# Second batch's first layer: the block method twice in three of four slot pairs, its weight sums made one pair ahead, its input sums in idle tiles

## The chip, the cores and the metric

The kernel runs on one core of a Trainium2 chip. The metric is the device time of one execution in microseconds. All times below are from runs of the kernel before on that core, and times within an execution are counted from the start of its profiled span.

## The reference

Two blocks follow each other. The first is attention in which a query sees only the keys that are assigned to the same cluster:

```
mask = q_assign[:, :, :, None] == k_assign[:, :, None, :]
scores = where(mask, scale * q @ k.T, -1e9)
x = softmax(scores) @ v            # 4 batches, 8 heads, 768 rows, 64 columns
```

Its result, with the heads side by side, is a matrix x of 3072 rows and 512 columns. The second block is two layers:

```
h = x @ w_in                       # 512 x 2048
g = h * (1 / (1 + exp(-1.702 * h)))
out = g @ w_out                    # 2048 x 512
```

All data are fp32. The change concerns the first of these two layers, for the second of the four batches of 768 rows.

## The kernel before, in words

The kernel first runs the attention of all four batches, and then, batch by batch (b = 0 to 3), the first layer and the second layer. Each layer is done by a block method of Strassen's kind: a product of 2 x 2 blocks is made from seven block products instead of eight, at the price of sums of blocks of the weights, of the input and of the results. In the third and fourth batch (b = 2, 3) the method is used twice in the first layer: of the seven outer products, four are again split into 2 x 2 blocks with seven products each.

**Slots.** The first layer's 2048 columns are 16 groups of 128 (`NF`), taken as `FB` = 8 slots; slot f gives the columns of groups f and f + 8. A pair j (0 to 3, `FQ` = 4 of them) joins the slots j and j + 4. The rows of a batch are two halves of 384 (`HALF`), each two quarters of 192 (`QT`). The result lies in the tile G.

**The first batch** (b = 0) runs `first7` for each slot.

**The second batch** (b = 1) runs `first7_psum` for each slot, in the order `TURN` = 0, 4, 1, 5, 2, 6, 3, 7. It makes seven products of two matmuls of 384 columns, into three PSUM banks x, z and v. Several products are added into a bank that has been copied out just before: the third, fifth and seventh into x, the sixth into v. ScalarE copies the banks out (L942, L946, L949) and applies the gelu (`finish`, L936); VectorE adds (`add`, L884). ScalarE's order in a slot is: copy of the first product, copy of the third, gelu of g1[0] (which needs VectorE's add of z), copy of v, gelu of g2[1] (which needs VectorE's add of x), and so on. Between the slots VectorE makes the weight sums of a later slot (`sums_w1`, three sums of 256 columns) and, after each second slot, the eight sums that the method needs a second time for a whole pair (`inner_w`). These are not used in this batch; they are written to DRAM (`kept_i`, four transfers, 1.5 MB for each pair) for the two batches that follow. `after7` makes a difference of two results and, for the second slot of a pair, `start_t`, the first input sums of the second layer, in the tiles Y11, E0, E1 and E2.

**The third and fourth batch** run `first49`. For each pair j it makes three outer products with full halves (`whole`, products 1, 6 and 7, four matmuls of 384 columns each, in two banks of the pool of two named m) and seven inner products (`inner`, four matmuls of 192 columns each, in six banks b: two each of z, x and v). Inner products go in the order 2, 1, 5, 6, 3, 7, 4; the adds of 3 and 7 are VectorE's, the copies of the others ScalarE's. The order of everything is written out by hand in the loop over j: the wholes of pair j − 1 stand between the inner products of pair j, except in the first pair, which has all three wholes of its own at its start, and the last, which has its own at its end. Weight sums come from `kept_i` through `load_inner` into the tiles Zb; the sixteen sums of the input M are made first of all, on VectorE. The function hands back a generator `rest`, two steps that are run in the first block of the second layer.

**What sets the order.** The instruction order of each engine is the order of the program text. Each engine takes its instructions in that order, and the SP queue its transfers. Small steps are woven between others with generators: `do(steps, n)` runs the next n steps. `pend` holds three steps that turn the previous batch's result (two VectorE transposes each, into E0, E1 and E2) and store it (four transfers each).

**The second layer** (`second49`, seven blocks k) uses weight sums `W[k]`, each of three transfers of 256 KB from `kept_w` (`load_sums`), in a pool of two buffers. `load_sums(0)` and `load_sums(1)` for the second batch are issued in the blocks 5 and 6 of the first.

Of the kernel before, what the change touches and what calls it, by code (L numbers as in the profile page):

```python
# [38 lines left out]
def fast(  # L39
# [789 lines left out]
    def load_sums(k, made=False):  # L829
        W[k] = ws.tile([P, 3, FQ, P], FP32, name="Wz")  # L830
        if made:
            keep_w(k, [W[k][:, i] for i in range(3)], nc.vector)
            return
        for i in range(3):
            nc.sync.dma_start(out=W[k][:, i], in_=kept_w[k, i])
# [86 lines left out]
    def first7_psum(b, f, X, T):  # L922

        S = w_of.pop(b * FB + f)

        def product(ps, a, x, start=True):
            for c in range(2):
                nc.tensor.matmul(out=ps, lhsT=a[:, c], rhs=x(c),  # L928
                                 start=start and c == 0, stop=(c == 1),
                                 skip_group_check=True)  # L930

        def bank_b():
            return ps_b.tile([P, 512], FP32, name="b")[:, 0:HALF]

        def finish(g, ps=None):
            nc.scalar.activation(out=g, in_=g if ps is None else ps,  # L936
                                 func=AF.Gelu_apprx_sigmoid, scale=2.0)

        g1, g2 = G[:, f], G[:, f + FB]
        x, z, v = (bank_b() for _ in range(3))  # L940
        product(x, A_in(0, 0, f), lambda c: X[0, 0, c])
        nc.scalar.copy(g1[:, 0], x)  # L942
        product(z, A_in(0, 1, f), lambda c: X[1, 0, c])
        add(g1[:, 0], z, g1[:, 0])
        product(x, S[2], lambda c: T[2, c], False)
        nc.scalar.copy(g1[:, 1], x)  # L946
        finish(g1[:, 0])
        product(v, S[1], lambda c: T[1, c])
        nc.scalar.copy(g2[:, 1], v)  # L949
        product(x, S[3], lambda c: T[3, c], False)  # L950
        add(g2[:, 1], x, g2[:, 1])
        finish(g2[:, 1])
        product(v, S[4], lambda c: X[1, 1, c], False)
        add(g1[:, 1], v, g1[:, 1])
        finish(g1[:, 1])
        product(x, A_in(1, 1, f), lambda c: T[4, c], False)
        finish(g2[:, 0], x)
# [19 lines left out]
    def sums_w1(n):  # L977

        if n >= FB:
            return  # L980
        f = TURN[n]
        if n not in range(2, 6):
            S = wq.tile([P, 3, 2, P], FP32, name="W")
        else:
            S = Zb[1 + n // 2 % 2][:, n % 2 * 6:n % 2 * 6 + 6].rearrange(
                "p (i c) n -> p i c n", c=2)
        w_of[FB + f] = {1: S[:, 0], 2: S[:, 1], 3: A_in(1, 0, f), 4: S[:, 2],
                        0: S}
        S = w_of[FB + f]
        A11, A12, A22 = A_in(0, 0, f), A_in(0, 1, f), A_in(1, 1, f)  # L990
        sums(nc.gpsimd if n < 2 else nc.vector, (
            (S[2], A22, "-", S[3]), (S[1], S[2], "+", A11),
            (S[4], A12, "-", S[2])))

    def inner_w(j, S):

        st = Zb[4]
# [9 lines left out]
        for n, (a, s3) in enumerate(((of_s, st[:, 0:2]),  # L1007
                                     (of_w, of_w(1, 0)))):
            s2, s1, s4 = (st[:, i:i + 2] for i in range(2 + 6 * n, 8 + 6 * n, 2))
            sums(nc.vector, ((s3, a(0, 0), "-", a(1, 0)),  # L1010
                             (s2, a(1, 1), "-", s3),
                             (s1, s2, "+", a(0, 0)),
                             (s4, a(0, 1), "-", s2)))
        for at, x in ((slice(0, 14), st[:, 0:14]),
                      (slice(14, 20), S[0].rearrange("p i c n -> p (i c) n")),
                      (slice(20, 22), S[1][:, 1]),
                      (slice(22, 24), S[1][:, 0:3:2, 1])):
            nc.sync.dma_start(out=kept_i[j, :, at], in_=x)

# [10 lines left out]
    def first49(X, T):  # L1030
# [5 lines left out]
        rooms = [tq[:, i] for i in range(2)]  # L1036
        for _ in range(2):
            r = wq.tile([P, 3, 2, P], FP32, name="W").rearrange(
                "p i c n -> p (i c n)").rearrange("p (n t) -> p n t", t=QT)
            rooms += [r[:, i] for i in range(4)]  # L1040
        rooms += [ep.tile([P, QT], FP32, name="p5") for _ in range(2)]
        M = {}
        for o in b:
            M[o] = {1: b[o][0, 0], 2: b[o][1, 0], 3: b[o][1, 1],
                    7: b[o][0, 1], **{n: rooms.pop(0) for n in (6, 5, 4)}}
        for todo in ((2, 5), (3, 4)):
            for n, one, op, two in ((7, 3, "-", 7), (6, 7, "+", 1),
                                    (5, 3, "-", 6)):
                for o in todo:
                    sums(nc.vector, ((M[o][n], M[o][one], op, M[o][two]),))  # L1050
        for o in b:
            sums(nc.vector, ((M[o][4], M[o][2], "-", M[o][6]),))

# [18 lines left out]
        def whole(j, n):  # L1072
# [3 lines left out]
            for m in range(2):  # L1076
                f = j + m * FQ
                at = j % 2 * 8 + m * 4
                a = {1: A_in(0, 0, f), 6: Zb[4][:, at:at + 2],
# [22 lines left out]
        def inner(j, n):  # L1102
# [7 lines left out]
            def a(o):  # L1110
# [7 lines left out]
                elif o == 5:  # L1118
                    known = {1: K[:, 14], 2: K[:, 15], 4: L[:, 6], 7: K[:, 0]}
                    s2 = 2  # L1120
                else:
                    known = {1: L[:, 2], 2: L[:, 3], 4: L[:, 7], 7: K[:, 1]}
                    s2 = 3
# [33 lines left out]

        end = FQ - 1
        for j in range(FQ):
            if j == 0:  # L1160
                whole(0, 1)
                inner(0, 2)
                p1 = keep_whole(0)
                whole(0, 6)
                u2 = keep_whole(0)
                inner(0, 1)
                do(pend, 3)
                whole(0, 7)
            else:
# [3 lines left out]
                if j > 1:  # L1173
                    whole(j - 1, 6)
                    add_whole(j - 1, 0, 1)
                load_inner(j + 1, (1,))
            inner(j, 5)
            if j < end:
                inner(j, 6)
            if j:  # L1180
                if j > 1:
# [7 lines left out]
            if j:  # L1189
# [5 lines left out]
            inner(j, 7)  # L1195
            if j == end:
                whole(j, 6)
                u2 = keep_whole(j)
            elif j:
                whole(j, 1)  # L1200
            inner(j, 4)
            if j == end:
                whole(j, 7)
            load_inner(j + 2, (0,))
# [3 lines left out]
            if j:  # L1208
                add_whole(j, 0, 0)
                close(j - 1)  # L1210
            else:
                for h, o in enumerate((p1, u2)):
                    g = quarter(0, 0, h)
# [162 lines left out]

    oks = {}
    pend = iter(())
    for b in range(B):
        if b == 1:  # L1380
            done = None
            for n, f in enumerate(TURN):
                made_w = w_of[FB + f][0]
                first7_psum(b, f, *XT)
                if n % 2 == 0 and done:
                    inner_w(*done)
                sums_w1(n + 2)
                if n:
                    after7(TURN[n - 1])
                if n % 2 == 0:  # L1390
                    one = made_w
                else:
                    done = f - FQ, (one, made_w)
                do(pend, 2)
            after7(FB - 1)
            inner_w(*done)
        if b > 1:
            rest = first49(*XT)
# [41 lines left out]
        def chain(*todo):  # L1440
            for steps in todo:
                yield from steps

# [6 lines left out]
        if b < 2:  # L1450
            rest = iter(())

        for k in range(7):
# [19 lines left out]
            if k < 5:  # L1473
                load_sums(k + 2, b == 0 and k > 2)
            elif b < B - 1:
# [452 lines left out]
```

## Time and profile before

| what | us |
|---|---|
| median of 3 runs (888.67 to 888.92) | 888.7 |
| the profiled execution | 888.23 |
| its span, first to last instruction | 886.1 |
| second batch's first layer, from the first L928 matmul to the first L1254 matmul | 476.21 to 549.78 |
| second batch's second layer | 549.9 to 613.6 |
| third batch's first layer | 613.48 to 681.11 |
| third batch's second layer | 681.2 to 744.9 |

The page is that of one execution. PE is TensorE, PEld its weight loads, DVE VectorE, ACT ScalarE, POOL GpSimd, and SP the engine that issues most transfers. A matmul in fp32 has two records, each with its own weight load. The matmuls' ends are modelled and overlap the next one's start, so that the distance between starts, and not the printed length, is what a matmul costs. A bracket after a timeline line gives how long the engine was idle before it, and what ended that idle time.

### The profile page before, as it was taken

To read this page: it belongs to the slowest core of one execution; us is meant where nothing else is said; L and a number is where in the kernel's file an instruction comes from. 1 tells how busy PE (TensorE), PEld (TensorE's weight loads), DVE (VectorE), ACT (ScalarE), POOL (GpSimd) and SP (SyncE) were. 2 spreads that over 40 slices of the span, in tenths; PEclk is the share of its full clock that TensorE was granted. 3 is DMA by queue.
4 is the path that set the end of the run, shared out by engine and by line. 5 is a ranking of instruction groups with operands and counts; after the bars stand their busy time and mean duration, and the time that the engine had idled before them with its cause. 6 is when DMAs were issued, how large, how long until landed. Compare 5 with 4: busy or idle time off the path is not lost.

```text
span 886.1 us, 18197 instructions
## 1 busy us (share of the span) xinstructions
PE 873.0 (99%) x6910; PEld 604.4 (68%) x6910; DVE 727.3 (82%) x1241; ACT 394.5 (45%) x868; POOL 430.9 (49%) x393
## 2 busy tenths in 40 slices
PE   8999999999999999999999999999999999999996
PEld 3444444444444445557997556999888998887996
DVE  4899899999999996999798556799666899665994
ACT  3677777777677774222112333111444212444211
POOL 6899999999999998695220000134000143000120
PEclk9999999999999999999999999999999999999999
DMA  9755566665656220024643321747501547501523
GB/s 172 136 107 106 104 121 137 137 147 128 137 131 136 87 68 19 0 107 143 221 150 112 103 93 71 285 144 268 170 26 48 171 145 260 173 25 48 187 65 99
DMA packets 183185, 110.48 MB, mean 125 GB/s; under 512 B 153528, under 2 KB 161712, under 8 KB 180528
## 3 DMA queue, kind: packets, MB, share of 16 engines
q1 hardware_dynamic: 182832, 109.09, 45.5%
q8 instruction: 57, 0.93, 0.5%
q14 instruction: 40, 0.33, 0.1%
q10 hardware_dynamic: 256, 0.13, 0.1%
HBM read 83.05 MB, written 26.14 MB: 123 GB/s over the span
## 4 chain that ended last, share of the span: by engine, by line
PE 95%; DVE 2%; DMA 1%; SPq 1%; ACT 0%; issue 0%; POOL 0%; DVEq 0%; ACTq 0%
PE b L1254 29%; PE s L492 14%; PE o L557 14%; PE b L1129 8%; PE b L893 8%; PE m L1084 7%; PE b L928 6%; PE s L515 3%; PE m L574 3%; PE m L348 1%; DVE Z L618 1%; DMA in<-in_q_dram 1%; SPq L134 0%; DMA short<-in_centroids_dram 0%; DVE G L884 0%
## 5 line engine op out<-in xcount | busy, mean ns | idle before, releaser
L541 POOL TENSOR_TENSOR sum<-sum,A 128x384 f32<-128x384 f32 x252 | 265.2, 1087 | 23.2 <-ACT A L523 21.5
L618 POOL TENSOR_TENSOR Y<-y,Y 128x768 f32<-128x768 f32 x24 | 59.8, 2503 | 384.8 <-DVE y L884 357.5
L523 ACT ACTIVATE A<-s 128x768 f32<-128x768 f32 x192 | 146.0, 807 | 86.0 <-PE s L515 64.7
L492 PE MATMUL s<-T,T 64*64 64x384 f32 x1536 | 143.1, 487 | 0.0
L557 PE MATMUL o<-A,inv 64*64 64x384 f32 x1536 | 141.2, 483 | 0.0
L884 DVE TENSOR_TENSOR G<-b,G 128x384 f32<-128x384 f32 x128 | 68.4, 554 | 52.5 <-PE b L928 29.3
L492 PEld LDWEIGHTS s<-T,T 64*64 64x64 f32 x1536 | 54.9, 132 | 69.1 <-ACT A L523 35.8
L618 DVE TENSOR_TENSOR G<-G 128x768 f32<-128x768 f32 (+1 forms) x84 | 99.3, 1209 | 0.2
L557 PEld LDWEIGHTS o<-A,inv 64*64 64x64 f32 x1536 | 58.3, 133 | 38.4 <-issue 33.3
L1254 PE MATMUL b<-G,w_out 128*128 128x192 f32 x320 | 55.9, 326 | 0.0
L1142 ACT COPY G<-b 128x384 f32<-128x384 f32 x64 | 30.4, 479 | 52.2 <-PE b L1129 52.2
L1254 PEld LDWEIGHTS b<-G,w_out 128*128 128x128 f32 x320 | 52.7, 190 | 1.1
L1254 PE MATMUL b<-E,Wz 128*128 128x192 f32 x288 | 50.3, 326 | 0.0
L1254 PEld LDWEIGHTS b<-E,Wz 128*128 128x128 f32 x288 | 47.3, 190 | 0.3 <-DVE E L618 0.3
L515 PE MATMUL s<-rows,rows 64*64 64x384 bf16 x720 | 45.4, 322 | 0.0
L515 PEld LDWEIGHTS <-rows 64*64 64x64 bf16 x720 | 23.0, 107 | 32.7 <-issue 32.7
L1254 PE MATMUL b<-G,Wz 128*128 128x192 f32 x224 | 41.0, 326 | 0.0
L1254 PE MATMUL b<-G,Z 128*128 128x192 f32 x224 | 39.0, 326 | 0.0
L541 POOL TENSOR_TENSOR sum<-A 128x384 f32<-128x384 f32 x32 | 37.3, 1185 | 0.0
L1254 PEld LDWEIGHTS b<-G,Wz 128*128 128x128 f32 x224 | 37.2, 190 | 0.0
L898 ACT ACTIVATE G<-G 128x384 f32<-128x384 f32 x32 | 16.1, 523 | 46.5 <-DVE G L884 45.1
L1254 PEld LDWEIGHTS b<-G,Z 128*128 128x128 f32 x224 | 36.8, 190 | 0.0
(237 smaller groups left out, 1681.1 us busy)
## 6 DMA issues: line engine op xcount, KB each, us to landing
Wz<-kept_w SPq DMA_DIRECT2D x78, 256.0 KB
Z<-kept_z SPq DMA_DIRECT2D x9, 1024.0 KB
raw<-in_moe_w_in_dram SPq DMA_DIRECT2D x16, 512.0 KB
raw<-in_moe_w_out_dram SPq DMA_DIRECT2D x16, 512.0 KB
Z<-kept_i SPq DMA_DIRECT2D x8, 1024.0 KB
inv<-in_v_dram SPq DMA_DIRECT2D x16, 384.0 KB
in<-in_q_dram SPq DMA_DIRECT2D x60, 96.0 KB
in<-in_k_dram SPq DMA_DIRECT2D x60, 96.0 KB
```

The lines of the kernel that those rows point to most:

```text
L492: nc.tensor.matmul(out=ps[c:c + D, a, 0:HALF], lhsT=T[p, 1][rows, kt * P + c:kt * P + c + D], rhs=T[p, 0][rows, h * HALF:(h + 1) * HALF], ...
L515: nc.tensor.matmul(out=s_of[u][c:c + D, a, :], lhsT=rows_of[1, p % 2][rows, kt * P + c:kt * P + c + D], rhs=rows_of[0, p % 2][rows, h * HA ...
L523: nc.scalar.activation(out=A_of[u], in_=s_of.pop(u), func=AF.Exp, scale=SCALE)
L541: nc.gpsimd.tensor_tensor(out=sum_of[g][:, a], in0=(A_of[u - 1] if kt == 1 else sum_of[g])[:, a], in1=A_of[u][:, a], op=ALU.add)
L557: nc.tensor.matmul(out=o_of[g][a * D:(a + 1) * D, r, 0:HALF], lhsT=v_in[p][rows, a, kt, :], rhs=A[rows, a, :], start=(kt == 0), stop=(kt = ...
L618: engine.tensor_tensor(out=o, in0=a, in1=b, op=(ALU.add if op == "+" else ALU.subtract))
L884: nc.vector.tensor_tensor(out=o, in0=p, in1=a, op=ALU.add)
L893: nc.tensor.matmul(out=ps[:, 0:HALF], lhsT=a[:, c], rhs=x(c), start=(c == 0), stop=(c == 1))
L928: nc.tensor.matmul(out=ps, lhsT=a[:, c], rhs=x(c), start=start and c == 0, stop=(c == 1), skip_group_check=True)
L1084: nc.tensor.matmul(out=whole_of[j][m][:, 0:HALF], lhsT=a[:, c], rhs=x(c), start=n == 1 and c == 0, stop=c == 1, skip_group_check=True)
L1129: nc.tensor.matmul(out=ps[i][:, h * QT:(h + 1) * QT], lhsT=a(o), rhs=M[o][n], start=n in (1, 2, 5) and h == 0, stop=True, skip_group_check ...
L1254: nc.tensor.matmul(out=ps, lhsT=A[n][:, f], rhs=M[n][:, f], start=start and f == 0, stop=(f == FQ - 1), skip_group_check=True)
```

## The change

In the second batch only the slots 0 and 4 are still made by `first7_psum`. The pairs 1, 2 and 3 are made by `first49`, which now takes the first pair `j0`, the input sums `M`, the weight sums `own` and background steps `bg`.

- **Weight sums.** `make_w(j)` makes the three sums of each of the pair's two slots (six of 256 columns; for pair 0 they exist) and the eight inner ones, and writes them to `kept_i` with the same four transfers. It is a generator with a step after each sum. The sums of pair j + 1 are made during pair j: `back` runs two steps after each inner product and the rest at the pair's end. Those of pair 1 are made during the slots 0 and 4, those of pair 0, which only later batches need, during pair 3. Their places are Y12 and Y21, or Zb[4], for the slots' sums, and Zb[1] or Zb[2] for the inner ones.
- **First two slots.** `first7_psum` calls a hook after the matmuls of each product, ahead of that product's add. The hook runs two steps of a chain: `pend`, `make_w(1)`, and the sixteen input sums (`sums_m`). What is left of the chain is run after the second slot.
- **Input sums.** They lie in the tile of W[1], which is taken in the first batch's last block but not loaded there, in Y22, in tq and in two p5 tiles. `load_sums(1)` is issued after the first layer.
- **Rest.** The second batch's second layer now runs the `rest` steps in its first block, as the later batches do.

The diff, cut to its core:

```diff
-    def first7_psum(b, f, X, T):
+    def first7_psum(b, f, X, T, hook):
...
                                  start=start and c == 0, stop=(c == 1),
                                  skip_group_check=True)
+            hook()
...
-        sums(nc.gpsimd if n < 2 else nc.vector, (
-            (S[2], A22, "-", S[3]), (S[1], S[2], "+", A11),
-            (S[4], A12, "-", S[2])))
-
-    def inner_w(j, S):
-
-        st = Zb[4]
+    def sums_s(f, S, engine):
+
+        A11, A12, A22 = A_in(0, 0, f), A_in(0, 1, f), A_in(1, 1, f)
+        for o, x, op, y in ((S[:, 1], A22, "-", A_in(1, 0, f)),
+                            (S[:, 0], S[:, 1], "+", A11),
+                            (S[:, 2], A12, "-", S[:, 1])):
+            sums(engine, ((o, x, op, y),))
+            yield
+
+    def make_w(j):
+
+        if j == 2:
+            own[j] = [Zb[4][:, m * 6:m * 6 + 6].rearrange(
+                "p (i c) n -> p i c n", c=2) for m in range(2)]
+        elif j:
+            own[j] = [Y[n].rearrange("p a t -> p (a t)").rearrange(
+                "p (i c n) -> p i c n", c=2, n=P) for n in (12, 21)]
+        S, st = own[j], Zb[1 if j == 0 else 1 + j % 2]
+        for m in range(2 if j else 0):
+            yield from sums_s(j + m * FQ, S[m], nc.vector)
...
+            for one in ((s3, a(0, 0), "-", a(1, 0)), (s2, a(1, 1), "-", s3),
+                        (s1, s2, "+", a(0, 0)), (s4, a(0, 1), "-", s2)):
+                sums(nc.vector, (one,))
+                yield
...
-    def first49(X, T):
+    def first49(X, T, M, own, bg, j0):
...
+        def back(j, n=2):
+            if own:
+                do(bg[j], n)
...
-        for j in range(FQ):
+        for j in range(j0, FQ):
+            first, late = j == j0, j > j0 + 1
...
+            back(j)
             inner(j, 5)
+            back(j)
             if j < end:
                 inner(j, 6)
+                back(j)
...
             inner(j, 3)
+            back(j)
...
             inner(j, 7)
+            back(j)
...
             inner(j, 4)
+            back(j)
...
+            back(j, 16)
...
         if b == 1:
-            done = None
-            for n, f in enumerate(TURN):
-                made_w = w_of[FB + f][0]
-                first7_psum(b, f, *XT)
-                if n % 2 == 0 and done:
-                    inner_w(*done)
-                sums_w1(n + 2)
-                if n:
-                    after7(TURN[n - 1])
-                if n % 2 == 0:
-                    one = made_w
-                else:
-                    done = f - FQ, (one, made_w)
-                do(pend, 2)
-            after7(FB - 1)
-            inner_w(*done)
+            M = {}
+            rooms = in_rooms(W[1].rearrange("p i f n -> p (i f n)")) + in_rooms(
+                Y[22].rearrange("p m t -> p (m t)")) + more_rooms()
+            bg = {j: make_w(j + 1) for j in range(1, FQ - 1)}
+            bg[FQ - 1] = make_w(0)
+            bg[0] = chain(pend, make_w(1), sums_m(*XT, rooms, M))
+            for f in (0, FQ):
+                first7_psum(b, f, *XT, lambda: do(bg[0], 2))
+            after7(0)
+            do(bg[0], 40)
+            after7(FQ)
+            rest = first49(*XT, M, own, bg, 1)
+            load_sums(1)
         if b > 1:
-            rest = first49(*XT)
+            rest = first49(*XT, {}, None, None, 0)
...
             if k < 5:
                 load_sums(k + 2, b == 0 and k > 2)
+            elif (b, k) == (0, 6):
+                W[1] = ws.tile([P, 3, FQ, P], FP32, name="Wz")
             elif b < B - 1:
                 load_sums(k - 5)
```

## The prediction

> **What bounds the kernel now.** First the page's busy line and the chain that ended last.
>
> ```profile
> PE 873.0 (99%) x6910; PEld 604.4 (68%) x6910; DVE 727.3 (82%) x1241; ACT 394.5 (45%) x868; POOL 430.9 (49%) x393
> PE 95%; DVE 2%; DMA 1%; SPq 1%; ACT 0%; issue 0%; POOL 0%; DVEq 0%; ACTq 0%
> ```
>
> TensorE is nearly always busy and is 95% of the chain, so time falls only by fewer matmul passes or fewer stalls. The chain in order of time puts the second batch's first layer between 476.21 and 549.78 us: 73.57 us. Then busy times by stretch: two of its slots, and the third batch's first layer, which already runs the method that the change brings.
>
> ```profile
> 494.50:503.60 9.10, 9.10 (x29) 5.32 (x28) 4.22 (x11) 3.46 (x8) 0.00 (x0) 1.00 0.20 43
> 503.60:512.70 9.10, 8.70 (x28) 4.88 (x27) 6.91 (x18) 2.96 (x7) 0.00 (x0) 1.00 0.45 173
> 613.60:681.20 67.60, 67.60 (x322) 54.56 (x321) 42.30 (x93) 28.84 (x53) 0.00 (x0) 1.00 0.28 85
> ```
>
> The columns are stretch, length, then busy us of PE, PEld, DVE, ACT and POOL. PE is full except where DVE has a burst of weight sums (6.91 us of 9.10). The timeline shows how that burst reaches PE:
>
> ```profile
> 504.72 0.42 DVE L618 TENSOR_TENSOR Z<-w_in 128x256 f32<-128x256 f32 x1
> 505.18 0.43 DVE L618 TENSOR_TENSOR Z<-Z,w_in 128x256 f32<-128x256 f32 x1
> 505.52 0.42 DVE L618 TENSOR_TENSOR Z<-w_in,Z 128x256 f32<-128x256 f32 x1
> ...
> 508.78 0.55 DVE L884 TENSOR_TENSOR G<-b,G 128x384 f32<-128x384 f32 x1
> 509.37 0.52 ACT L936 ACTIVATE G<-G 128x384 f32<-128x384 f32 x1 [1.52 <-DVE G L884]
> 509.80 0.46 ACT L949 COPY G<-b 128x384 f32<-128x384 f32 x1
> 510.31 1.56 PE L928 MATMUL b<-x,Z 128*128 128x384 f32 x4 [0.40 <-ACT G L949]
> ```
>
> The add (L884) stands behind the sums; the gelu (L936) waits for the add; the copy that empties the bank (L949) stands behind the gelu; the next accumulating product waits for the copy. This chain decides the prediction.
>
> [...] the copy at 509.80 did not pass the gelu. [...] The trace has 0.42 and 0.35. [...] the trace has starts closer than durations: eleven 256-wide sums started from 502.68 to 506.99, 0.39 us apart. I use 0.39, 0.47 for 384-wide, 0.27 for the independent 192-wide, 0.88 to 0.91 for 768-wide.
>
> **PE work removed.** A dense slot of L928 takes 9.03 us (485.24 to 494.27). Eight are 72.24; the two burst slots took 9.70 (503.30 to 513.00), 1.34 more in all, which gives the 73.58 seen. After: two slots stay, 18.06. The other three pairs run as the third batch does. From its timeline: first pair 17.11 (613.48 to 630.59), second 11.68 (to 642.27), last 22.00 (659.11 to 681.11); the pair between, 16.84, is not needed. Sum 50.79. Undisturbed, the stage takes 68.85: **4.72 us less**.
>
> **DVE work moved and added.** The old method used DVE for 41.4 us of 73 (eight stretches). The new one needs, by the third batch, about 8.4 us per pair of 16.9 (42.3 less 5.7 of input sums and 2.9 of output transposes, over four), and the change puts a further 14 sums of 256 into each pair's idle places (eight in the last): 14 x 0.39 = 5.5. DVE is then about 80% full and in one order. What matters is where the sums stand. From the built program's instruction order I walk DVE forward; four places bind.
>
> *First slot.* Before, the first add of z started at 479.06. Now six transposes of the old output (starts 0.47 apart, from 478.98) and one sum go first: add at 482.25 to 482.81. Gelu, then copy of v at 483.28, ends 483.74. The sixth product, due at 482.66, starts near 483.79: 1.13 lost. The add that the seventh product needs stands behind six further sums: 482.72 + 6 x 0.39 = 485.06, ends 485.62; the product is due at 485.08: 0.54 lost. At 510.31 the restart itself cost 0.1 (1.39 to the next product against 1.29), so two restarts: in all **1.87**. The second slot's adds find DVE free.
>
> *First pair, inner(4).* It waits for inner(7)'s adds. In the third batch:
>
> ```profile
> 627.34 2.44 DVE L884 TENSOR_TENSOR G<-b,G 128x384 f32<-128x384 f32 x4 [2.05 <-PE b L1129]
> ...
> 629.18 0.59 PE L1129 MATMUL b<-W,w_in 128*128 128x192 f32 x2
> ```
>
> Two adds, then two more, and PE starts as the third ends. Two sums now stand between them: **0.65**.
>
> *Second pair, whole(1).* From here DVE never idles. Counted from the pair stage's start: inner(7)'s adds end their turn at 16.69; six sums 19.03; 768-wide adds (0.88 + 2 x 0.91) 21.73; two adds 22.67; six sums 25.01; the third add_whole ends 26.5. That add frees the first bank for whole(1), due at 24.91 + 0.65 = 25.56 (in the third batch 638.39, where the bank had been free for 2 us). **1.08** with the restart.
>
> *Last pair, whole(6) and whole(7).* The same queue goes on: adds, two sums, adds, six sums, 768-wide add, bank free at 33.3 against 33.12 due; then 37.35 against 37.33. **0.43** with restarts. After that, wholes stand between every dependence and the queue drains.
>
> Added stalls: 1.87 + 0.65 + 1.08 + 0.43 = **4.0 us**. Stage: 68.85 + 4.03 = 72.88; gain 73.57 − 72.88 = **0.7 us**.
>
> **What I cost at nothing, and its cover.** Input sums: ten of sixteen lie in the second slot, six before the pairs, first needed by inner(5), 10.3 us into the pairs; cover gone, they cost 0.27 each. Pool: it makes the same two slots' sums as before. SP: the twelve output stores come about 6 us earlier; eight took 5.7 us from issue to end of traffic, so twelve end near 489, and start_t, which overwrites the same E tiles, comes at 498; every SP transfer behind them (sixteen kept_i pieces) has longer before its tile is reused. The wait that moves is W[1]'s load: formerly started at 475, now after the last inner(4), 2.6 us before the second layer, behind 1.57 MB of kept_i. Its first third is needed at 11.7 us of the layer; 1.83 MB in some 14 us asks for 130 GB/s, and the queue moved 217 to 466 GB/s in the slices from 555 to 565 us. The end moved into the second layer (rest) is as in the third batch, whose layer takes 63.70 as the second batch's does.
>
> Restart costs and the 0.47 of adds are read from single places; each stall could be 0 (if a start lies a few tenths otherwise) or twice its size. So the stalls span 0 to 8 us, and I take the walk.
>
> **Forecast.** The profiled execution took 888.23 (span 886.1 and 2.1 around it): 887.5 after. The median, 888.7, lies 0.5 higher: **888.0**.
>
> **Rivals.**
> *The cover holds.* The third batch runs the pairs with a total wait of 0.3 us; if DVE recovers before each dependence, all 4.7 us come: 884.0. For it: DVE has 25 us idle in that stage. Against: the idle time lies mostly after inner(4) and in the late wholes, not ahead of the banks. Half the stalls would give 886.0.
> *DVE falls further behind: slower.* Twenty-two sums stand in the unbroken queue from the first pair to the last whole(7), and seven ahead of the first slot's two stalls. If a sum takes its turn in p, the stalls grow by 29 (p − 0.39): parity at 0.415, 2.5 us slower (891) at 0.50. For it: while Pool worked, two 384-wide in-place sums took 2.2 us each (607.39). Against: Pool is idle in this stage, and starts there lay at 0.34 to 0.45.
> *W[1] late: slower.* Below 130 GB/s the second layer waits; at the 85 GB/s of the third batch's first layer it would be 7 us, 895. That rate is demand, not a limit.
>
> **Chances.** Less than 0.2% (1.8 us) is about what a measurement of this kernel can tell from no change. Forecast and its near neighbours, 886.9 to 890.5: 0.63. Cover holds, wholly or for the most part: 0.24. DVE further behind: 0.10; W[1]: 0.03. So faster 0.24, same 0.63, slower 0.13. The range leaves out about a tenth on each side: 885.7 to 889.9.
>
> **What would show it.** Records of L929 should be 56, of the whole products 72 more, of the inner ones 168 more. Right: first slot near 10.9 us with waits for L951's copy and a DVE add; PE waits of about a microsecond ahead of the second pair's whole(1), released by a DVE add from m; DVE over 80% busy between. Wrong: pairs of 17.1, 11.7, 22.0 (then 884), or a PE wait on DMA at the second layer's second product, or 256-wide sums starting over 0.45 apart.

## The result, and the profile after

The changed kernel took 887.03 us (median of 13 runs, 886.55 to 887.47) beside 888.92 for the kernel before: a ratio of 0.9977, 95% interval [0.9968, 0.9985]. In two further comparisons it took 887.20 and 887.22 us. A gain of 0.7 was forecast (888.7 to 888.0); the three comparisons give 1.9, 1.1 and 1.4, about twice as much. That is small, but each interval leaves out 1. The profiled execution took 887.47 us, of which 885.6 are span.

First the page's busy line and the chain that ended last.

```profile
PE 871.5 (98%) x6982; PEld 613.9 (69%) x6982; DVE 744.1 (84%) x1277; ACT 398.8 (45%) x870; POOL 431.1 (49%) x393
PE 96%; DVE 3%; issue 0%; ACT 0%; POOL 0%; DVEq 0%; ACTq 0%; POOLq 0%
```

TensorE (PE) is busy for 1.5 us less, although it has 72 more instructions: the inner products are smaller and more numerous. VectorE (DVE) is busy for 16.8 us more. TensorE's timeline dates the stage: the first L929 matmul starts at 476.39 and the first of the second layer (L1309) at 548.66, 72.27 us, where the kernel before took 73.57. The gain in the stage is 1.30 us; 0.69 was forecast. In the repeats the stage took 72.29 and 72.30.

Now the stretches: the first slot, the second pair and the second layer behind the stage (columns as in the prediction).

```profile
476.40:485.60 9.20, 8.19 (x26) 4.31 (x25) 9.10 (x24) 1.90 (x5) 0.00 (x0) 1.00 0.33 69
513.80:526.40 12.60, 12.06 (x66) 10.55 (x66) 12.41 (x28) 6.79 (x13) 0.00 (x0) 1.00 0.34 126
548.80:612.50 63.70, 63.70 (x394) 63.70 (x393) 60.42 (x77) 13.28 (x37) 19.18 (x8) 1.00 0.64 215
```

In the first slot and in the second pair VectorE has no gap (9.10 of 9.20, 12.41 of 12.60) and TensorE has: the sign that the prediction asked for. Between the two VectorE is not full, though: from 485.60 to 513.80 it is busy for 18.25 of 28.20 us, where the prediction asked for over 80%. In the second layer nothing waits. The same thing in the timeline of TensorE, at the four places where it stands still for more than a tenth:

```profile
483.76 1.56 PE L929 MATMUL b<-x,W 128*128 128x384 f32 x4 [0.76 <-ACT G L951]
485.57 1.56 PE L929 MATMUL b<-Tx,w_in 128*128 128x384 f32 x4 [0.25 <-DVE G L885]
...
512.37 0.59 PE L1168 MATMUL b<-Wz,w_in 128*128 128x192 f32 x2 [0.68 <-DVE G L885]
...
522.28 2.85 PE L1115 MATMUL m<-x,w_in 128*128 128x384 f32 x8 [0.54 <-DVE G L885]
```

They are the first slot's sixth and seventh product, the first pair's inner(4) and the second pair's whole(1), each released by the add or the copy that was named. The bracket counts idle time by modelled ends; what a wait costs is read from the starts. The prediction's fourth place, the last pair, shows no bracket, but its whole(6) and whole(7) start 0.05 and 0.07 us late, each right behind the VectorE add that frees their first bank, and each is followed by a restart (2.68 us to the next product instead of 2.58):

```profile
528.99 2.85 PE L1115 MATMUL m<-Tx,Z 128*128 128x384 f32 x8
...
533.04 2.85 PE L1115 MATMUL m<-Tx,w_in 128*128 128x384 f32 x8
```

In the first slot VectorE's timeline shows what stands ahead of the two adds (L885), six transposes and a sum ahead of one, six sums ahead of the other:

```profile
479.15 2.87 DVE L1399 STREAM_TRANSPOSE E<-Y 128x384 f32<-128x384 f32 x6
481.94 0.38 DVE L618 TENSOR_TENSOR Y<-w_in 128x256 f32<-128x256 f32 x1
482.24 0.55 DVE L885 TENSOR_TENSOR G<-b,G 128x384 f32<-128x384 f32 x1
...
484.96 0.55 DVE L885 TENSOR_TENSOR G<-b,G 128x384 f32<-128x384 f32 x1
```

In the second pair the chain in order of time leads from the wait at 522.28 back through VectorE alone as far as 510.50, an add of inner(3); its "issue" pieces are 0.30 us at most. Its end:

```profile
515.04 3.54 DVE G L885 x5
...
519.29 0.76 DVE Y L618 x2
...
520.75 1.49 DVE G L885 x3
522.24 0.04 issue
522.28 2.85 PE m L1115 x8
```

Five adds, then six weight sums (L618), then the adds that free the bank, then TensorE.

### The profile page after: what moved, and what is told of

Read it like the earlier page. It is cut to its first block, busy times and chain, and to the rows that moved or that the text cites. A ratio compares the mean times of both kernels' runs of the same rounds, so it can differ in the third digit from the quotient of the medians.

```text
span 885.6 us, 18392 instructions
## 1 busy us (share of the span) xinstructions
PE 871.5 (98%) x6982; PEld 613.9 (69%) x6982; DVE 744.1 (84%) x1277; ACT 398.8 (45%) x870; POOL 431.1 (49%) x393
## 4 chain that ended last, share of the span: by engine, by line
PE 96%; DVE 3%; issue 0%; ACT 0%; POOL 0%; DVEq 0%; ACTq 0%; POOLq 0%
PE b L1309 28%; PE s L492 14%; PE o L557 14%; PE b L1168 10%; PE m L1115 10%; PE b L894 8%; PE s L515 3%; PE m L574 3%; PE m L348 1%; PE b L929 1%; DVE G L885 1%; PE o L296 1%; DVE Y L618 0%; PE s L506 0%; DVE Z L618 0%
## 5 line engine op out<-in xcount | busy, mean ns | idle before, releaser
L618 POOL TENSOR_TENSOR Y<-y,Y 128x768 f32<-128x768 f32 x24 | 59.8, 2505 | 385.2 <-DVE y L885 361.3
L618 DVE TENSOR_TENSOR G<-G 128x768 f32<-128x768 f32 (+1 forms) x81 | 98.9, 1248 | 0.1
L885 DVE TENSOR_TENSOR G<-b,G 128x384 f32<-128x384 f32 x128 | 67.9, 553 | 33.1 <-PE b L1168 15.3
L1181 ACT COPY G<-b 128x384 f32<-128x384 f32 x88 | 41.8, 480 | 70.6 <-PE b L1168 70.6
L1309 PE MATMUL b<-G,w_out 128*128 128x192 f32 x320 | 55.9, 326 | 0.0
L1309 PEld LDWEIGHTS b<-G,w_out 128*128 128x128 f32 x320 | 52.7, 190 | 1.1
L1309 PE MATMUL b<-E,Wz 128*128 128x192 f32 x288 | 50.3, 326 | 0.0
L1309 PEld LDWEIGHTS b<-E,Wz 128*128 128x128 f32 x288 | 47.3, 190 | 0.3 <-DVE E L618 0.3
L1099 ACT ACTIVATE G<-G 128x768 f32<-128x768 f32 x44 | 36.4, 844 | 14.6 <-DVE G L885 14.2
L885 DVE TENSOR_TENSOR G<-m,G 128x384 f32<-128x384 f32 x64 | 32.0, 549 | 11.2 <-PE m L1115 11.2
L1309 PE MATMUL b<-G,Wz 128*128 128x192 f32 x224 | 41.0, 326 | 0.0
L1309 PE MATMUL b<-G,Z 128*128 128x192 f32 x224 | 39.0, 326 | 0.0
L1309 PEld LDWEIGHTS b<-G,Wz 128*128 128x128 f32 x224 | 37.2, 190 | 0.0
```

The lines of the kernel that those rows point to most:

```text
L618: engine.tensor_tensor(out=o, in0=a, in1=b, op=(ALU.add if op == "+" else ALU.subtract))
L885: nc.vector.tensor_tensor(out=o, in0=p, in1=a, op=ALU.add)
L1181: nc.scalar.copy(o, halves(ps[i]))
L1309: nc.tensor.matmul(out=ps, lhsT=A[n][:, f], rhs=M[n][:, f], start=start and f == 0, stop=(f == FQ - 1), skip_group_check=True)
```

## The experiments

The theory, called A where the expectations name it: each of these stalls is an add that stands in VectorE's single order behind background steps, or a ScalarE copy that waits for such an add, so the number and the place of the steps ahead set the wait, and the TensorE work that the change removes is all there. Its rivals put a wait down to something else at its place, or hold that the work taken away from one place comes due at the next. All stage times below run from the first L929 (L928) matmul to the first of the second layer, in the profiled execution; the "slots" part ends, and the "pairs" part begins, with the first whole product's first matmul. Undisturbed they would be 18.06 + 50.79 = 68.85 by the prediction (its 50.79 is read from the third batch and so holds that batch's 0.3 us of waits); the changed kernel has 19.60 + 52.67 = 72.27.

**The change as it is, again** (a0_after, a1_after), beside two of the sets below.

> The changed kernel once more, beside the kernel before and the next three on one chip, so that they can be compared with it. Both theories: 1.3 to 1.9 us faster than before, first layer of the second batch near 72.3 us.

> The change as it is, on the same chip as the two. Stage 72.3 us, 887.0 to 887.3 beside 888.3 to 888.9 of before.

Measured: 887.20 us (21 runs) beside 888.30, ratio 0.9986 [0.9980, 0.9993]; and 887.22 (20 runs) beside 888.63, ratio 0.9984 [0.9977, 0.9991]. Of the gain the stage gives 1.3. Another 0.3 lies outside the span: an execution takes 1.75 to 1.94 us more than its span in every run of the change, and 2.13 to 2.24 in every run of the kernel before for which the span is on record.

**The hooks after the adds** (e1_hooks_after_adds). The background steps of the two slots run behind the adds of a slot and not ahead of them.

```diff
                                  skip_group_check=True)
-            hook()
...
         add(g1[:, 0], z, g1[:, 0])
+        for _ in range(2):
+            hook()
...
         add(g2[:, 1], x, g2[:, 1])
+        for _ in range(3):
+            hook()
...
         add(g1[:, 1], v, g1[:, 1])
+        for _ in range(2):
+            hook()
```

> The hook's steps of the two first slots stand after VectorE's adds (two, three and two steps' worth after the adds of z, x and v) instead of ahead of them; everything else is as in the changed kernel. My theory (in the first slot the adds stand behind transposes and weight sums, ScalarE's copy of v behind the gelu that waits for the add): the two waits of the first slot go, the two slots take 18.1 us instead of 19.6, the kernel is 1.5 us faster than the changed one. Rival (VectorE is short of time in these slots as a whole): the wait comes back at the second slot or at the first pair, and the time is that of the changed kernel, within 0.3 us.

Measured: 885.57 us, ratio 0.9963 [0.9949, 0.9976] to before, 1.6 below the change in the same set. VectorE now makes the add of z first:

```profile
479.34 0.56 DVE L885 TENSOR_TENSOR G<-b,G 128x384 f32<-128x384 f32 x1
479.81 2.87 DVE L1404 STREAM_TRANSPOSE E<-Y 128x384 f32<-128x384 f32 x6
```

TensorE's timeline of the first slot, where x4 is one product and x8 two:

```profile
482.94 1.45 PE L929 MATMUL b<-x,W 128*128 128x384 f32 x4
484.23 1.45 PE L929 MATMUL b<-Tx,w_in 128*128 128x384 f32 x4
485.52 2.74 PE L929 MATMUL b<-x,w_in 128*128 128x384 f32 x8
```

Starts lie 1.29 apart and no row has a bracket. The slots take 18.06 (476.49 to 494.55), exactly the undisturbed time, against 19.60; the pairs stay at 52.68. The same steps in the same number cost nothing when the add goes first, and no wait came back later. The first slot's stall was the place of the transposes and sums.

**Two sums moved from between the adds to behind them** (e2_sums_after_7).

```diff
             inner(j, 3)
-            back(j)
...
             inner(j, 7)
-            back(j)
+            back(j, 4)
```

> The two weight sums between the adds of inner(3) and inner(7) are moved behind those of inner(7), in every pair; nothing else changes. Theory A (VectorE's queue is unbroken from there to the second pair's whole(1), so its length decides): the 0.65 us wait ahead of the first pair's inner(4) goes, and the wait ahead of the second pair's whole(1) grows by as much or up to 0.3 us more: the time stays within 0.3 us of the changed kernel's. Theory B (each wait has its own cause in the order at its place): 0.65 us faster.

Measured: 887.80 us (21 runs), ratio 0.9994 [0.9987, 1.0001]. The pairs took 53.24 (495.64 to 548.88), 0.57 more than in the change: the first pair 0.68 less (17.11), the second 1.04 more (13.60), the last 0.21 more (22.53). Neither theory gave that: A had allowed 0.3 more, B had 0.65 less. The wait of inner(4) went, and whole(1) of the second pair waits longer, in TensorE's timeline:

```profile
522.37 2.85 PE L1115 MATMUL m<-x,w_in 128*128 128x384 f32 x8 [1.28 <-DVE G L885]
```

The stall was passed on, and more with it. VectorE's timeline shows where most of the addition comes from. The changed kernel first:

```profile
509.85 1.21 DVE L885 TENSOR_TENSOR G<-b,G 128x384 f32<-128x384 f32 x2 [2.57 <-PE b L1168]
510.98 0.41 DVE L618 TENSOR_TENSOR Z<-Z 128x256 f32<-128x256 f32 x1
511.43 0.43 DVE L618 TENSOR_TENSOR Z<-Z,Z 128x256 f32<-128x256 f32 x1
511.77 1.02 DVE L885 TENSOR_TENSOR G<-b,G 128x384 f32<-128x384 f32 x2
...
514.96 0.95 DVE L885 TENSOR_TENSOR G<-G 128x768 f32<-128x768 f32 x1
```

And the experiment:

```profile
509.50 2.44 DVE L885 TENSOR_TENSOR G<-b,G 128x384 f32<-128x384 f32 x4 [2.58 <-PE b L1168]
511.86 0.42 DVE L618 TENSOR_TENSOR Z<-Z 128x256 f32<-128x256 f32 x1
...
515.04 0.95 DVE L885 TENSOR_TENSOR G<-G 128x768 f32<-128x768 f32 x1
```

From the first add to the 768-wide add it is 5.11 us in the changed kernel and 5.54 here, with the same instructions. Four adds in a row take 2.36, where four at 0.47 would be 1.88: the later two wait for TensorE's products. The two sums had filled most of that hole; moved out, they lengthen the queue by 0.43, and whole(1) starts 0.44 later after the pairs' start (26.73 for 26.29). So part of the stall at inner(4) bought work that would cost time elsewhere.

**Slot sums on GpSimd** (e3_slot_sums_on_pool): those of pairs 2 and 3, six each, leave VectorE.

```diff
-            yield from sums_s(j + m * FQ, S[m], nc.vector)
+            yield from sums_s(j + m * FQ, S[m],
+                              nc.vector if j == 1 else nc.gpsimd)
```

> The six slot sums of the pairs 2 and 3 are made by GpSimd, which is idle in this stage, instead of VectorE; the eight inner sums stay. Theory A (VectorE's queue is too long by itself): six sums of 0.39 us leave the queue ahead of the second pair's whole(1), the waits there and at the last pair's wholes go, about 1.1 us faster than the changed kernel; the wait ahead of the first pair's inner(4) stays. Rival (GpSimd's sums hold VectorE up, as in the second layer, where two in-place sums of 384 took 2.2 us each while GpSimd worked): VectorE's sums lengthen beside them, and the time is that of the changed kernel or up to 2 us more.

Measured: 888.35 us (13 runs), ratio 0.9997 [0.9989, 1.0005]: no gain, and 1.2 over the change, within what the rival said. Yet the stage took only 70.02 us (481.41 to 551.43), with slots of 18.47 and pairs of 51.55. It began 5.0 us late (in the profiled execution, 889.59 us, the longest of its runs). GpSimd's order, as its timeline shows, has nothing ahead of pair 2's sums that would hold them, so they were made in the first batch's second layer:

```profile
456.86 1.44 POOL L618 TENSOR_TENSOR Z<-w_in 128x256 f32<-128x256 f32 x1
```

And VectorE beside them:

```profile
457.63 1.21 DVE L618 TENSOR_TENSOR Wz<-w_out 128x512 f32<-128x512 f32 x1
...
461.04 0.35 DVE L885 TENSOR_TENSOR y<-b,y 128x192 f32<-128x192 f32 x1
```

The weight sum took 1.21 us; in the changed kernel the same one, at 456.43, took 0.68. The add of a PSUM bank (b) to a tile kept its 0.35. In that stretch VectorE fell from 1.2 us behind the changed kernel (457.63 against 456.43) to 3.9 behind (the next transposes, 465.50 against 461.62), and TensorE waited 2.3 us for it at 464.06:

```profile
464.06 2.38 PE L1310 MATMUL b<-Tx,Wz 128*128 128x192 f32 x8 [2.28 <-DVE Tx L618]
466.23 2.35 PE L1310 MATMUL b<-E,Wz 128*128 128x192 f32 x8
```

The wait was not all that this cost. The sixteen matmuls behind it took 4.35 us (464.06 to 468.41), where the change's took 2.68 (460.71 to 463.39). By their starts eight took 2.17 and the next eight 2.18, against 1.30 ahead of the wait (455.12 to 456.42 in the same timeline) and 1.30 afterwards (468.41 to 469.71). So of the 5.0 us, 1.2 were there before, 2.1 are the longer wait and 1.7 the slower matmuls.

Not all of the shorter stage is the edit's gain. TensorE came to the slots 5.0 us later than in the change, VectorE's transposes only 3.9 later (483.04 against 479.15), so the first slot waited 1.1 less without any edit there. The other 1.1 are the pairs, as the theory had it; the edit lost more elsewhere.

**Pair 3's slot sums alone on GpSimd** (e4_pair3_sums_on_pool). Their tiles, Y12 and Y21, are read by the first pair's whole products, which holds them back to 501 us.

```diff
-            yield from sums_s(j + m * FQ, S[m], nc.vector)
+            yield from sums_s(j + m * FQ, S[m],
+                              nc.gpsimd if j == 3 else nc.vector)
```

> Only the six slot sums of pair 3, whose places (Y12 and Y21) are not free before the end of pair 1, are made by GpSimd; those of pair 2 are VectorE's again. In the run before, GpSimd, which waits for nothing there, made pair 2's sums some 50 us early, in the middle of the full second layer of the first batch, and VectorE and the products lost time there; the pair stage itself became 1.1 us shorter. Theory A (the loss was that early start, the pair stage is short of VectorE time): no loss ahead of the stage, waits ahead of the second pair's whole(1) and the last pair's wholes gone, about 0.9 us faster than the changed kernel. Rival (GpSimd slows VectorE wherever both work): at least as slow as the changed kernel, VectorE's sums beside GpSimd's well over 0.42 us.

Measured: 886.07 us (8 runs) beside 888.44, ratio 0.9975 [0.9965, 0.9986]. The pairs took 51.54 (495.97 to 547.51), 1.13 less than in the change. The waits of whole(1), whole(6) and whole(7) are gone: from inner(4) on, the chain in order of time holds TensorE alone.

```profile
512.35 9.45 PE b L1169 x56
521.79 2.58 PE m L1116 x8
```

Six sums fewer ahead of the bank, and the bank is free in time. The sums that ran beside GpSimd's were again slowed, in VectorE's timeline, but stood ahead of nothing urgent:

```profile
513.80 0.84 DVE L618 TENSOR_TENSOR Z<-w_in 128x256 f32<-128x256 f32 x1
514.67 0.83 DVE L618 TENSOR_TENSOR Z<-Z,w_in 128x256 f32<-128x256 f32 x1
```

**The kernel before with its bursts spread** (e5_before_spread). Eight `first7_psum` slots as before, but the eight inner sums of a pair are made two at a time, behind the adds.

```diff
-                first7_psum(b, f, *XT)
-                if n % 2 == 0 and done:
-                    inner_w(*done)
+                first7_psum(b, f, *XT, lambda: do(bg, 2))
+                if n % 2:
+                    do(bg, 20)
...
         add(g1[:, 0], z, g1[:, 0])
+        hook()
```

> The kernel before, with the eight inner sums of a pair no longer in one burst but two at a time after each of VectorE's adds of the next two slots; the same products as before. Theory A (of the changed kernel's gain a part, 1.3 us, is that the two bursts of the kernel before are gone, and only the rest comes from fewer products less new waits): 1.3 us faster than before, slots all 9.03 us. Rival (the bursts cost nothing that spreading returns, the gain is the products' alone): as before, within 0.3 us.

Measured: 887.27 us (21 runs), ratio 0.9986 [0.9979, 0.9993]. The stage is one unbroken piece of the chain:

```profile
476.55 72.24 PE b L928 x224
```

72.24 is eight times the dense slot of 9.03. The bursts cost the kernel before 1.3 us, and spreading them, without any new method, takes the whole kernel to the change's time (887.0 to 887.2 in its three comparisons).

**All three edits** (e6_all_three): e1, e2 and e4 together.

> Three moves together on the changed kernel: hook steps after the adds in the two first slots, the two sums between the adds of inner(3) and inner(7) behind those of inner(7), and pair 3's slot sums on GpSimd. Theory (the waits named in the prediction are all the stage loses): nearly all of them go, the stage takes about 69.0 us against 72.3, the kernel is 3.3 us faster than the changed one and 4.5 to 5 us faster than before. Rival (what is saved at one place comes back at the next): no more than 2.2 us faster than the changed kernel.

Measured: 885.09 us, ratio 0.9962 [0.9949, 0.9976]; slots 18.06, pairs 52.10, stage 70.16: 1.2 more than expected. That is about 2.1 us below the change (measured in other comparisons), so by the number the rival was right: part of what was saved came back. New waits stand at the second pair's start, 0.36 at 514.70 for a VectorE sum and 0.44 at 517.98 for a copy. The last of pair 2's inner sums, put off by the e2 edit, now lie beside GpSimd's work, in VectorE's timeline:

```profile
511.14 2.16 DVE L618 TENSOR_TENSOR Z<-Z,Z 128x256 f32<-128x256 f32 x3
```

With e2 alone the same three took 1.22.

**Half-wide sums** (e8_half_sums). Every weight sum that VectorE makes for the pairs is cut to half its columns. The kernel leaves the other half out, so its results are not usable; only its time counts here.

```diff
+            one = (o, x, op, y)
+            if engine is nc.vector:
+                one = (o[:, 0:1], x[:, 0:1], op, y[:, 0:1])
+            sums(engine, (one,))
...
-                sums(nc.vector, (one,))
+                o, x, op, y = one
+                sums(nc.vector, ((o[:, 0:1], x[:, 0:1], op, y[:, 0:1]),))
```

> The changed kernel with every weight sum that VectorE makes for the pairs 0 to 3 cut to half its columns (the other half is left out, so that the products get old data there); order, waits and number of instructions stay. Theory (waits are paid by the length of the queue of sums): a sum takes its turn in about 0.27 us instead of 0.39, the first slot's waits shrink from 1.5 to about 1.0 us (the transposes stay), the first pair's from 0.7 to 0.4, the others go: 2.0 us faster than the changed kernel. Rival (the waits come from the order and the hand-over between engines, not from the sums' length): less than 0.7 us faster.

Measured: 884.98 us, ratio 0.9965 [0.9951, 0.9979]; slots 18.96, pairs 51.20, about 2.2 us below the change, near the theory's 2.0. Six sums between the two adds of the first slot, in VectorE's timeline, now take 1.33 (482.29 to 483.62), 0.22 each, where they took 2.25, 0.375 each; the 0.27 expected was an estimate. What is left of the waits, in TensorE's:

```profile
483.35 1.56 PE L929 MATMUL b<-x,W 128*128 128x384 f32 x4 [0.63 <-ACT G L951]
...
511.18 0.59 PE L1172 MATMUL b<-Wz,w_in 128*128 128x192 f32 x2 [0.41 <-DVE G L885]
```

The sixth product keeps its wait, since ahead of its add stand six transposes and one sum, and only the sum became shorter. The seventh product, with six sums ahead, and the whole products wait no longer. Inner(4), with two sums ahead, should wait 2 x (0.375 − 0.22) = 0.3 less than 0.68, and waits 0.41. These waits follow the sums that stand ahead of them, by number and length.

**Two edits together** (e9_hooks_and_pool): e1 and e4, without e2. **And the first pair's two sums put off** (e10_and_first_pair): the same, with

```diff
             inner(j, 3)
-            back(j)
+            back(j, 0 if first else 2)
...
             inner(j, 7)
-            back(j)
+            back(j, 4 if first else 2)
```

> The two edits that gained by themselves, together: in the slots 0 and 4 the background steps run after the adds, and the six slot sums of pair 3 are GpSimd's; the two sums between the adds of the products 3 and 7 stay where the change put them. Theory (each stall has its own place in VectorE's order, so that gains add): slots 18.06 us, pairs 51.5 as with the GpSimd edit alone, stage 69.5 us against 72.3 of the change; 2.7 us less than the change, about 884.3 beside 888.4 of before. Rival (the adds of the slots gain their place at the cost of later sums, as the sums beside GpSimd take twice as long): a new wait at the second pair's first inner products, as when all three edits were made, stage 70.1 or more, 885.1 or more.

> As the one before, and in the first pair alone the two sums between the adds of the products 3 and 7 go behind those of 7. Theory: the wait of the first pair's inner(4), 0.6 us, goes too, and as the queue of the second pair is now shorter by GpSimd's six sums, nothing comes due in its place: stage 68.9 us, 0.6 less than the one before. Rival: the sums put off are the ones that the second pair's inner products wait for, so the wait comes back there: stage within 0.2 us of the one before, or above it.

Measured: e9 884.37 us beside 888.63 of before, ratio 0.9953 [0.9939, 0.9967]; slots 18.06, pairs 51.55, stage 69.61. This is the fastest version, 2.8 us below the change, as the theory expected. One wait is left in its stage, in TensorE's timeline, that of inner(4):

```profile
510.91 0.59 PE L1174 MATMUL b<-Wz,w_in 128*128 128x192 f32 x2 [0.68 <-DVE G L885]
```

e10 took 884.99 us, ratio 0.9958 [0.9944, 0.9971], pairs 52.10: 0.55 worse in the stage, so its rival was right. TensorE's timeline has the wait again, at the products that read the sums put off:

```profile
515.74 0.56 PE L1174 MATMUL b<-Wz,Z 128*128 128x192 f32 x2 [0.35 <-DVE Z L618]
519.02 1.24 PE L1174 MATMUL b<-x,Z 128*128 128x192 f32 x6 [0.45 <-ACT G L1187]
```

In e9 the last two sums are done when GpSimd begins; in e10 three of them share the time with it. VectorE and GpSimd, e9 first:

```profile
511.24 0.75 DVE L618 TENSOR_TENSOR Z<-Z,Z 128x256 f32<-128x256 f32 x2
...
511.96 0.94 POOL L618 TENSOR_TENSOR Y<-Y,w_in 128x256 f32<-128x256 f32 x1 [7.93 <-issue]
```

```profile
512.18 2.16 DVE L618 TENSOR_TENSOR Z<-Z,Z 128x256 f32<-128x256 f32 x3
...
512.27 0.92 POOL L618 TENSOR_TENSOR Y<-Y,w_in 128x256 f32<-128x256 f32 x1 [7.26 <-issue]
```

The stages side by side, in us:

| kernel | slots | pairs | stage | median |
|---|---|---|---|---|
| undisturbed, by the prediction | 18.06 | 50.79 | 68.85 | – |
| the kernel before | – | – | 73.57 | 888.3 to 888.9 |
| the change | 19.60 | 52.67 | 72.27 | 887.0 to 887.2 |
| e1, hooks after the adds | 18.06 | 52.68 | 70.74 | 885.57 |
| e2, two sums put off | 19.61 | 53.24 | 72.85 | 887.80 |
| e3, sums of pairs 2 and 3 on GpSimd | 18.47 | 51.55 | 70.02 | 888.35 |
| e4, pair 3's sums on GpSimd | 19.60 | 51.54 | 71.14 | 886.07 |
| e5, the kernel before, bursts spread | – | – | 72.24 | 887.27 |
| e6, e1 + e2 + e4 | 18.06 | 52.10 | 70.16 | 885.09 |
| e8, half-wide sums | 18.96 | 51.20 | 70.16 | 884.98 |
| e9, e1 + e4 | 18.06 | 51.55 | 69.61 | 884.37 |
| e10, e9 with two sums put off | 18.06 | 52.10 | 70.16 | 884.99 |

## Why the prediction was right, and where its sizes were off

**TensorE work removed, 4.72 us: right.** e5 shows the old method without waits at 72.24, e1 the two slots at 18.06. e9 has 69.61 with one wait of 0.68, that is 68.93 without it, where the prediction had 68.85.

**The stalls: all four places right, the sum 0.6 too large.** It was forecast as 4.03 and is 72.27 − 68.85 = 3.42. Term by term:

- *First slot, forecast 1.87, measured 1.54.* The sixth product started 0.92 after its due time (482.84 to 483.76), not 1.13. Of that difference 0.09 is the single sum, which took its turn in 0.30 and not 0.39, and 0.06 is a slip in the prediction's own sum (478.98 + 6 x 0.47 + 0.39 is 482.19, not 482.25). The seventh lost 0.52 for 0.54. Of the two restarts at 0.1 only the second shows (485.57 to 486.96, 1.39 instead of 1.29), since the first is hidden in the wait that follows. The slot took 10.57 (476.39 to 486.96), where the prediction's sign said near 10.9. This is the term that was furthest off.
- *First pair, inner(4), forecast 0.65, measured 0.68.* The pair took 17.79 (495.99 to 513.78) for 17.11.
- *Second pair, whole(1), forecast 1.08, measured 0.88.* The pair took 12.56 for 11.68. The walk put the end of the last six sums at 25.01 after the pairs' start; they ended at 24.76, since a sum took its turn in 0.375 and not 0.39, twelve times, and the three 768-wide adds 2.60 and not 2.70. The product started 0.70 late; restarting cost 0.11, and inner(4) behind it another 0.07.
- *Last pair, forecast 0.43, measured 0.32* (22.32 for 22.00): two late starts of 0.05 and 0.07 and two restarts of 0.10.

**What was costed at nothing cost nothing.** No wait falls on the input sums. W[1]'s load was issued at 546.76, 1.9 us before the second layer and not 2.6, and the second layer took 63.70 (548.66 to 612.36), as before.

**The rivals.** *The cover holds* fell: TensorE started late at all four places. *DVE falls further behind* was decided by the turn of one sum, with parity at 0.415: it was 0.375, on the other side. *W[1] late* fell with the second layer's 63.70.

**From the profile to the median.** The forecast took 0.7 off the median and got 1.1 to 1.9. Of the difference 0.6 is the stalls, and 0.3 is time outside the span, which the prediction took as unchanged. It goes with the changed program: e5, the old method with its bursts spread, keeps the 2.1 to 2.2 of before, and every variant of the change has 1.75 to 1.94. What causes it is not shown. 1.3 and 0.3 make 1.6, inside 1.1 to 1.9, and the rest is scatter between comparisons. So 887.03 lies near the edge of the prediction's main range (886.9 to 890.5). That the profiled execution came out at 887.47, where 887.5 was forecast, is luck: from the third batch's first layer on it happened to take 0.6 us longer than the one before (273.24 for 272.62; 272.68 and 272.84 in the repeats).

Where did the expected gain go, then? The method removes 3.4 us from the dense old slots (72.24 − 68.85) and adds stalls of 3.4. What the change gains, 1.3 us, equals what the old kernel lost to its bursts (73.57 − 72.24). e1 and e4 together (e9) show that 2.7 of the 3.4 can be had by moving background steps alone.

## What to carry to other kernels

Background work on an engine that works in order, as VectorE did here (the add of z at 482.24 behind such work, at 479.34 ahead of it), is paid where something urgent stands behind it. In the first slot the place of the steps alone decided (e1, slots of 18.06 for 19.60), in the second pair, where VectorE has no gap, their number (e4, pairs of 51.54 for 52.67): put them behind the add that TensorE waits for, and count the steps ahead of each bank's release. Work that fills a hole of the engine's own can be cheap even if it delays the next add a little, so moving it can cost more than the delay (e2, pairs of 53.24). And before a new method is credited, spread the old one's bursts: here that alone gave as much as the new method did (e5).

## What the runs showed of the hardware

A VectorE sum of two SBUF tiles took longer while GpSimd also made sums: 0.83 or 0.84 us for 0.42 at 256 columns (e4), 1.21 for 0.68 at 512 and 1.21 and 1.36 for 0.95 and 0.96 at 768 (e3). An add with one input in PSUM kept its 0.35 (e3, 461.04), and two of 384 columns kept their 1.21 (e4, 503.79). GpSimd's own sums of 256 columns went from 0.72 or 0.73 to 0.90 to 0.94, though one kept its 0.73 (e4, 504.75), and to as much as 1.44 beside wider VectorE sums (e3). In e4, e9 and e10 every slowed run of VectorE sums of 256 columns ended 0.28 to 0.30 us after the GpSimd sum that it ran into. Whether VectorE stood still for that sum or worked more slowly beside it is not shown.

VectorE kept the order of the program text: the add of z started at 482.24 in the change, where it is written behind six transposes and a sum, and at 479.34 in e1, where it is written ahead of them. So did the SP queue: W[1]'s load began at 546.76, behind the four kept_i transfers written ahead of it (543.65 to 546.67).

Sums of 256 columns start 0.375 us apart on average (six from 482.71 to 484.96, six from 518.50 to 520.75), though each is printed as 0.41 to 0.43 long. One that reads the result of the sum just before it starts 0.44 to 0.46 after it, the others 0.33 to 0.35. The 0.42 and 0.35 in the prediction are such printed lengths, for 256 columns (504.72 in the kernel before) and 192 (507.46); it is the distance of starts that adds up in a queue. Restarting a stalled stream of matmuls cost 0.1 us: 1.39 for 1.29 between products of four, 2.69 for 2.58 between products of eight. Behind the one wait of 2.3 us (e3) sixteen matmuls took 4.35 us, and the same sixteen 2.68 in the change; behind the 1.28 us wait of e2 eight took 2.68 (522.37 to 525.05), 2.58 and a restart. What slowed the sixteen is not shown.
